# Bursts of three score tiles in a fused sigmoid attention and SiLU layer, with weighted counting of the work between them

## The chip, the cores and the metric

The kernel runs on one core of one Trainium2 chip. The metric is the device time of one execution in microseconds, the median of several runs. A profile of one execution gives the rows quoted below. Its engines are TensorE (PE, with its weight loads as PEld), VectorE (DVE), ScalarE (ACT), GpSimd (POOL) and SyncE (SP), whose queue issues DMAs.

## The reference

Two layers one after the other, in float32 at the borders. Attention has 8 batches, 12 heads, 448 positions and 64 columns per head; its weights are a sigmoid in place of a softmax. The second layer has 3,584 rows, 768 model columns and 2,048 hidden columns.

```python
scores = scale * np.matmul(q, k.transpose(0, 1, 3, 2)) - np.log(S)
attn = 1.0 / (1.0 + np.exp(-scores))
attn_out = np.matmul(attn, v)
x = attn_out.transpose(0, 2, 1, 3).reshape(B * S, H * D)
h = x @ w_in
g = h * (1.0 / (1.0 + np.exp(-h)))
out = g @ w_out
```

## The kernel before

The code writes every engine's order out by hand: the order of the Python calls is the order in each engine's queue, and TensorE, VectorE, ScalarE and the DMA queues each take their own instructions in that order. Tiles come from pools with a fixed number of buffers, and the waits between engines follow from who reads and writes them.

**Attention.** Heads are worked in 24 groups (three per batch, `g` from 0 to 23) of four heads. A group has 7 chunks, so there are 168 units `(g, ch)`; unit `n` belongs to group `n // 7`. `scores(g, ch)` (L170) issues eight 64x64 matmuls, two rounds of four that run side by side, into a score tile of two PSUM banks (pool `ps_sc`, two buffers), and one sigmoid over both banks on ScalarE into `attnT` (pool of 12). `values(g)` (L194) multiplies all seven `attnT` of a group with `v`: 28 matmuls in seven rounds, into two single banks (pool `ps_1`, four buffers). VectorE then empties these into `xT` (L219), and `after_values` starts later loads and queues the next rows.

**Rows to be transposed.** The scores need `k` and `q` with the head's columns on the partitions. Groups 0 to 5 are transposed on TensorE (`pe_transpose`). Groups 6 to 8 go by `dma_transpose` (L159) out of the h steps of batch 1. For group 9 and later, `after_values(g)` puts `(g + 3, "k")` and `(g + 3, "q")` into the list `later`, and `rows_if_any` (L467) takes one entry: VectorE copies the rows into another order (L163), and SP's queue issues the transposing DMA (L164) into `qkT`. With a `q` entry it also starts the load of a later group's k and q on POOL's queue.

**The second layer** is a stream of small steps, made by generators. `moe_h(b)` runs 16 h units for batch `b`; a unit is six 128x128 matmuls over 448 columns into one single bank (L236), a sigmoid `tsig` on ScalarE (L248) and a multiply on VectorE into `gTr` (L249). `out_set` (L289) makes two row blocks by two of the output with seven products in place of eight; a product is eight matmuls over 384 columns (L307). VectorE makes four sums and differences of blocks ahead (`S`) and adds the products up in `osb` (L315). The first product, M1, is emptied by ScalarE (L322). Two stores go to SP's queue after the sixth product and two after the seventh. The order is h0, h1, three sets, h2, a set, h3, three sets, and again from h4.

**The mix.** From unit 24 on, the main loop (L534) alternates bursts of two score tiles with a stretch of the stream. After the scores of a burst it runs the values of a waiting group, if there is one, and `rows_if_any`. `stretch(ns)` (L399) adds `ns` to `due` and takes steps until their counted time `done` reaches it: 189 per h step, 163 per product step. `hold` keeps a stretch going from the last h unit of a batch until M1 of the set behind it has been emptied. `paces` (L532) gives the time of a stretch by stage, `n // 21`. At unit 42 a stretch of 21,500 runs h1 through. What is left of the stream after the last burst runs as a dense tail.

## Time and profile before

| | |
|---|---|
| median of 3 runs | 382.31 us (382.2 to 382.5) |
| profiled execution | 382.75 us, span 381.0 |
| score matmuls, L177 | 672, busy 50.4 us, 362 ns each |
| values matmuls, L208 | 672, busy 37.9 us, 349 ns each |
| h matmuls, L236 | 768, busy 153.2 us, 353 ns each |
| sigmoid of a score tile, L184 | 168, busy 158.9 us |
| sigmoid `tsig`, L248 | 128, busy 68.2 us, 545 ns each |
| multiply into `gTr`, L249 | 128, busy 78.1 us, 623 ns each |
| additions into `osb`, L315 | 70 and 42, 555 and 552 ns each |
| M1's emptying, L322 | 14, 491 ns each |
| loads of q, k and v rows, POOL's queue | 112 KB each, 5.8, 5.5 and 4.8 us to landing |
| transposing DMAs into `qT`, SP's queue | 18, 6.2 us to landing (2.9 to 11.5) |
| stores of `osb`, SP's queue | 54, 2.9 us to landing |

Matmuls overlap in the array, so the duration of one is longer than the distance from one to the next; the distances come from the lengths of whole runs of matmuls in the chain of waits. A group's line names where the code issues it. "To landing" counts from the issue of a DMA to its last byte's arrival.

### The profile page before, as it was taken

The page shows a single profiled execution, that of the slowest core. Times are in us where ns is not written, and L with a number is a line of the kernel's source. Part 1 is how long each engine was busy: PE and PEld are TensorE (multiplying, and loading weights), DVE is VectorE, ACT ScalarE, POOL GpSimd, SP SyncE. Part 2 cuts the span into 40 slices and gives each one's busy share as a digit, 9 for nine tenths or more (in the row PEclk, how much of TensorE's full clock was granted, in tenths as well). Part 3 has the DMA queues.
Part 4 walks back from the last instruction along what each step waited for, and adds up shares of the span by engine and source line. Part 5 has one row for each costly group of instructions (what it writes and reads, how often), then busy time and mean ns, then how long its engine had stood idle before and what let it go on. Part 6 is the DMA issues. An engine that isn't in the chain of part 4 may idle for free.

```text
span 381.0 us, 7663 instructions
## 1 busy us (share of the span) xinstructions
PE 372.2 (98%) x3083; PEld 186.9 (49%) x3083; DVE 233.8 (61%) x415; ACT 240.0 (63%) x328; POOL 92.9 (24%) x158
## 2 busy tenths in 40 slices
PE   7999999999999999999999999999999999999995
PEld 2444445545554445444555444544455444555663
DVE  2446646996565666556767547735857446656773
ACT  4998886758777875778444686577774787044000
POOL 8855326202752323121311303101100000000000
PEclk9999999999999999999999999999999999999999
DMA  7999999974999936937939859535346300110233
GB/s 112 180 188 204 205 203 181 155 103 101 166 236 232 141 51 97 184 47 75 152 68 191 96 112 122 56 101 74 48 77 105 83 3 2 41 41 2 75 92 83
DMA packets 66403, 42.71 MB, mean 112 GB/s; under 512 B 37056, under 2 KB 62912, under 8 KB 66368
## 3 DMA queue, kind: packets, MB, share of 16 engines
q0 software_dynamic: 28032, 22.69, 42.7%
q1 hardware_dynamic: 38112, 19.31, 28.2%
q8 instruction: 24, 0.39, 0.4%
q10 hardware_dynamic: 224, 0.23, 0.2%
q14 instruction: 11, 0.09, 0.1%
HBM read 45.61 MB, written 11.01 MB: 149 GB/s over the span
## 4 chain that ended last, share of the span: by engine, by line
PE 80%; DMA 12%; DVE 2%; ACT 2%; POOL 1%; issue 1%; DVEq 0%
PE po L307 34%; PE ph L236 29%; PE psc L177 9%; PE pav L208 6%; DMA w_in_sb<-in_moe_w_in_dram 6%; DMA w_out_sb<-in_moe_w_out_dram 5%; DVE gTr L249 1%; DMA ks<-in_k_dram 1%; ACT attnT L184 1%; DMA vf<-in_v_dram 1%; DVE T L278 1%; POOL qf L78 1%; PE pw L135 1%; POOL kf L78 0%; ACT qr L138 0%
## 5 line engine op out<-in xcount | busy, mean ns | idle before, releaser
L184 ACT ACTIVATE attnT<-psc,bias_s 128x896 f16<-128x896 f32 x168 | 158.9, 1016 | 53.3 <-PE psc L177 53.2
L236 PE MATMUL ph<-xT,w_in_sb 128*128 128x448 f16 x768 | 153.2, 353 | 0.0
L249 DVE TENSOR_TENSOR gTr<-ph,tsig 128x448 f16<-128x448 f32 x128 | 78.1, 623 | 72.0 <-ACT tsig L248 71.4
L236 PEld LDWEIGHTS <-w_in_sb 128*128 128x128 f16 x768 | 71.9, 98 | 75.7 <-issue 12.9
L248 ACT ACTIVATE tsig<-ph 128x448 f16<-128x448 f32 x128 | 68.2, 545 | 47.8 <-PE ph L236 46.2
L78 POOL DMA_DIRECT2D vf<-in_v_dram x48 | 28.7, 613 | 140.7 <-PE pav L208 140.2
L307 PEld LDWEIGHTS <-S 128*128 128x128 f16 x448 | 42.3, 98 | 33.9 <-issue 6.8
L315 DVE SCALAR_TENSOR_TENSOR osb<-po,osb 128x384 f32<-128x384 f32 x70 | 37.7, 555 | 25.1 <-PE po L307 24.5
L177 PE MATMUL psc<-qT,kT 64*64 64x448 f16 x672 | 50.4, 362 | 2.5 <-ACT attnT L184 1.2
L219 DVE TENSOR_SCALAR xT<-pav 128x448 f16<-128x448 f32 x48 | 27.7, 619 | 30.3 <-PE pav L208 30.3
L307 PE MATMUL po<-T,S 128*128 128x384 f16 x224 | 40.6, 327 | 0.1
L307 PEld LDWEIGHTS <-gTr 128*128 128x128 f16 x304 | 28.7, 98 | 23.4 <-issue 5.2
L307 PE MATMUL po<-w_out_sb,S 128*128 128x384 f16 x224 | 39.9, 326 | 0.0
L208 PE MATMUL pav<-attnT,vf 64*64 64x448 f16 x672 | 37.9, 349 | 0.4 <-DVE gTr L249 0.4
L78 POOL DMA_DIRECT2D qf<-in_q_dram x48 | 28.9, 612 | 38.1 <-DVE qr L163 16.9
L307 PE MATMUL po<-w_out_sb,gTr 128*128 128x384 f16 x192 | 34.7, 327 | 0.0
L177 PEld LDWEIGHTS <-kT 64*64 64x64 f16 x672 | 15.0, 104 | 32.8 <-issue 30.9
L78 POOL DMA_DIRECT2D kf<-in_k_dram x48 | 28.9, 612 | 7.0 <-DVE kr L163 4.4
L208 PEld LDWEIGHTS <-vf 64*64 64x64 f16 x672 | 20.2, 107 | 12.4 <-issue 1.9
L315 DVE SCALAR_TENSOR_TENSOR osb<-po,m 128x384 f32<-128x384 f32 x42 | 23.2, 552 | 4.1 <-PE po L307 2.5
L322 ACT ACTIVATE m<-po 128x384 f32<-128x384 f32 x14 | 6.9, 491 | 23.7 <-PE po L307 23.7
L307 PE MATMUL po<-T,gTr 128*128 128x384 f16 x112 | 21.4, 326 | 0.0
(40 smaller groups left out, 131.0 us busy)
## 6 DMA issues: line engine op xcount, KB each, us to landing
out_dram<-osb SPq DMA_DIRECT2D x54, 192.0 KB, 2.9
qf<-in_q_dram POOLq DMA_DIRECT2D x48, 112.0 KB, 5.8
vf<-in_v_dram POOLq DMA_DIRECT2D x48, 112.0 KB, 4.8
kf<-in_k_dram POOLq DMA_DIRECT2D x46, 112.0 KB, 5.5
w_in_sb<-in_moe_w_in_dram POOLq DMA_DIRECT2D x4, 768.0 KB, 10.5
w_out_sb<-in_moe_w_out_dram POOLq DMA_DIRECT2D x4, 768.0 KB, 17.0
kT<-kr SPq DMA_TRANSPOSE x18, 5.6
qT<-qr SPq DMA_TRANSPOSE x18, 6.2
```

The costliest lines, as they stand in the source:

```text
L78: nc.gpsimd.dma_start(flat[name, g][half * HP : (half + 1) * HP, :, c0:c1].rearrange("p i c d -> p i (c d)"), source[name][b, h0 : h0 + 2] ...
L135: nc.tensor.matmul(pw, dummy[:, :P], dummy, start=True, stop=True)
L177: nc.tensor.matmul(psc[own, j, :S], qkT["k", g][rows, ch, own], qkT["q", g][rows, :, own], start=True, stop=True,)
L184: nc.scalar.activation(attnT[g, ch], psc[:, :, :S], AF.Sigmoid, bias=bias_s, scale=QKSCALE)
L208: nc.tensor.matmul(pav[half][j * D : (j + 1) * D, :S], flat["v", g][own, j, ch, :], at[own, j, :], start=(ch == 0), stop=(ch == NCH - 1),)
L219: nc.vector.tensor_scalar_mul(xT[b][:, half * NQ + iq, :], pav[half][:, :S], SX)
L236: nc.tensor.matmul(ph[:, :S], w_in_sb[:, cc, fc * P : (fc + 1) * P], xT[b][:, cc, :], start=(at == 0), stop=(at == NCC - 1),)
L248: nc.scalar.activation(tsig, ph[:, :S], AF.Sigmoid, bias=0.0, scale=ISX)
L249: nc.vector.tensor_mul(gTr[:, fc, (b % 2) * S : (b % 2) * S + S], ph[:, :S], tsig)
L307: nc.tensor.matmul(po[:, :NO2], a[:, fc, :], w[:, fc, :], start=(fc == 0), stop=(fc == NHC - 1))
L315: nc.vector.scalar_tensor_tensor(out=o, in0=po, scalar=sign, in1=x, op0=ALU.mult, op1=ALU.add)
L322: nc.scalar.activation(m1, po, AF.Copy, scale=ISX)
```

## The change

Bursts from unit 42 on have three tiles in stages 2 and 4 to 7 and two in stage 3, and two tiles whenever a group's values are waiting. In a burst of three the first tile goes to two single banks out of `ps_1`, with a sigmoid for each, the second and third to `ps_sc`, and the third's sigmoid is put off: it is issued behind the next `tsig` or M1's emptying, or once a stretch has taken steps of more than 1,300 ns, or at the stretch's end. `stretch` counts a step by a weight: 0.72 in the h stages from batch 2 on, 1.28 in the sets. `hold` begins an h unit earlier from batch 2 on. The paces change, and a stretch is scaled by the tiles of its burst. Rows are no longer transposed in a burst that has a waiting group, unless more than one entry is queued at its start.

```diff
-    def scores(g, ch):
+    late = []
+
+    def late_sigmoid():
+        while late:
+            to, psc = late.pop()
+            nc.scalar.activation(to, psc, AF.Sigmoid, bias=bias_s, scale=QKSCALE)
+
+    def scores(g, ch, banks=None, put_off=False):
         attnT[g, ch] = p12.tile([P, 2, S], F16, tag="attnT", name="attnT")
-        psc = ps_sc.tile([P, 2, 512], F32, tag="pssc", name="psc")
+        if banks is None:
+            psc = ps_sc.tile([P, 2, 512], F32, tag="pssc", name="psc")
+            banks = [psc[:, j] for j in range(2)]
+            parts = [(attnT[g, ch], psc[:, :, :S])]
+        else:
+            parts = [(attnT[g, ch][:, j], banks[j][:, :S]) for j in range(2)]
...
-        nc.scalar.activation(
-            attnT[g, ch], psc[:, :, :S], AF.Sigmoid, bias=bias_s, scale=QKSCALE
-        )
+        if put_off:
+            late.extend(parts)
+            return
+        for to, psc in parts:
+            nc.scalar.activation(to, psc, AF.Sigmoid, bias=bias_s, scale=QKSCALE)
+
+    def single_banks():
+        return [ps_1.tile([P, 512], F32, tag="ps1", name="psc1") for _ in range(2)]
...
     def h_unit(b, fc):
-        hold = b > 0 and fc == NFC - 1
+        weight = H_WEIGHT if b > 1 else 1.0
+        hold = b > 1 and fc >= NFC - 2 or b == 1 and fc == NFC - 1
...
         nc.scalar.activation(tsig, ph[:, :S], AF.Sigmoid, bias=0.0, scale=ISX)
+        late_sigmoid()
...
+    H_WEIGHT, SET_WEIGHT = 0.72, 1.28
...
     def out_set(a1, rows1, a2, rows2, last=False):
+        weight = SET_WEIGHT
...
         nc.scalar.activation(m1, po, AF.Copy, scale=ISX)
+        late_sigmoid()
...
     def stretch(ns):
         due += ns
+        since = 0
         while done < due or hold:
             step_ns = next(stream, None)
             if step_ns is None:
                 break
-            done += step_ns
+            done += step_ns * weight
+            since += step_ns
+            if since > 1300:
+                late_sigmoid()
+        late_sigmoid()
...
-    paces = {1: 1600, 2: 2000, 3: 2550, 4: 3400, 5: 3400, 6: 3000, 7: 3000}
+    TILES = {2: 3, 3: 2, 4: 3, 5: 3, 6: 3, 7: 3}
+    paces = {1: 1600, 2: 2400, 3: 2550, 4: 3500, 5: 3300, 6: 3100, 7: 2900}
+    def burst(n, tiles):
+        new = units[n : n + (tiles if not waiting else 2)]
+        for i, u in enumerate(new):
+            single = i == len(new) - 3
+            scores(*u, single_banks() if single else None, len(new) == 3 and i == 2)
+        rows = not waiting or len(later) > 1
+        values_if_any()
+        if rows:
+            rows_if_any()
+        waiting.extend(g for g, ch in new if ch == NCH - 1)
+        return len(new)
...
+    values_if_any()
+    stretch(21500)
+    n = 2 * NT_B
+    while n < len(units):
+        ns = paces[n // NT_B]
+        tiles = burst(n, TILES[n // NT_B])
+        n += tiles
+        stretch(ns * tiles / 2)
```

More of the change, by code (lines that the diff above doesn't have):

```diff
@@ L177, in scores @@
                 nc.tensor.matmul(
-                    psc[own, j, :S],
+                    banks[j][own, :S],
                     qkT["k", g][rows, ch, own],
@@ L228 @@
     hold = False
+    weight = 1.0
     def h_unit(b, fc):
-        nonlocal hold
-        hold = b > 0 and fc == NFC - 1
+        nonlocal hold, weight
+        weight = H_WEIGHT if b > 1 else 1.0
+        hold = b > 1 and fc >= NFC - 2 or b == 1 and fc == NFC - 1
         ph = ps_1.tile([P, 512], F32, tag="ps1", name="ph")
@@ L289, in out_set @@
     def out_set(a1, rows1, a2, rows2, last=False):
-        nonlocal hold
+        nonlocal hold, weight
+        weight = SET_WEIGHT
         lo, hi = slice(0, NHC), slice(NHC, NFC)
@@ L530 @@
             do(*what)
-    paces = {1: 1600, 2: 2000, 3: 2550, 4: 3400, 5: 3400, 6: 3000, 7: 3000}
-    stretch(paces[1])
-    for n in range(NT_B + 3, len(units), 2):
-        burst = units[n : n + 2]
-        if n == 2 * NT_B:
-            values_if_any()
-            stretch(21500)
-        for u in burst:
-            scores(*u)
-        values_if_any()
-        rows_if_any()
-        for g, ch in burst:
-            if ch == NCH - 1:
-                waiting.append(g)
+    TILES = {2: 3, 3: 2, 4: 3, 5: 3, 6: 3, 7: 3}
[11 more added lines that the diff above has]
+        return len(new)
+    stretch(paces[1])
+    for n in range(NT_B + 3, 2 * NT_B, 2):
+        burst(n, 2)
         if n in (24, 30):
@@ L549 @@
             transposes(4 + (n - 26) // 6, "q")
-        stretch(paces[1] if 1 not in ready else paces[n // NT_B])
+        stretch(paces[1])
+    values_if_any()
[6 more added lines that the diff above has]
+        stretch(ns * tiles / 2)
     for g in waiting:
```

## The prediction

> **What bounds the kernel now.** I read the busy times first, then the chain of waits in order of time, then the timeline around the transposing transfers, and last their landing times by stretch of the run.

> ```profile
> span 381.0 us, 7663 instructions
> ...
> PE 372.2 (98%) x3083; PEld 186.9 (49%) x3083; DVE 233.8 (61%) x415; ACT 240.0 (63%) x328; POOL 92.9 (24%) x158
> ```

> TensorE has work in 98% of the span; VectorE and ScalarE are idle over a third of it. Whatever adds idle time to TensorE adds it to the end. The chain of waits in order of time (start, duration, what) shows the rhythm, and the densest stretches at the end:

> ```profile
> 196.07 1.32 PE pav L208 x28
> 197.40 3.52 PE po L307 x21
> 200.92 0.50 PE psc L177 x8
> 201.42 3.52 PE po L307 x21
> ...
> 331.31 18.16 PE ph L236 x96
> 349.47 27.32 PE po L307 x168
> ```

> From these: one product matmul takes 27.32/168 = 0.163 us, one h matmul 18.16/96 = 0.189, one round of four 64x64 matmuls 1.32/7 = 0.189. A cycle of one burst of two score tiles and 21 products lasts 0.50 + 3.52 = 4.02 us, of which 21 x 0.163 + 2 x 0.189 = 3.79 are matmuls. The remaining **0.23 us** is what one change to 64x64 tiles and back costs. The 18-matmul cycles of the h stages (0.50 + 3.51) give the same 0.23.

> **Fewer bursts: a gain.** From unit 42 on there are 126 units. Before: 126/2 = 63 bursts. After, I walk the loop by hand: due grows by pace x tiles / 2, each h step counts 189 x 0.72 and each set step 163 x 1.28, a burst has two tiles whenever a group waits for its values, and the hold runs through two h units and M1. That gives 26 bursts of three and 24 of two, so 50. One pair of these (78 and 80, behind the hold after h2) has no step between them and shares one change. So 14 changes fewer: 14 x 0.23 = **3.2 us gained**. The steps in the tail are the same matmuls in another place: nothing.

> **ScalarE.** A split tile costs two activations of 0.533 us (68.2/128, tsig's row) in place of one of 0.946 (158.9/168): 26 x 0.12 = 3.1 us on an engine with 141 us idle. The tightest cycle is a burst of three and 17 products, 0.80 + 2.77 = 3.57 us, against 2 x 0.533 + 2 x 0.946 + about 0.15 for M1 = 3.1: it fits, so I take nothing. The put-off sigmoid holds its score bank until the next burst, at least 2.6 us on; tsig or M1 waits behind two tiles, as before. The one stall of TensorE behind scores in steady work (at 144.64, M1 and then four sigmoids in line, 0.65 us) shrinks by about **0.2**: the burst there now has 1.32 us of values between its two pairs of tiles.

> **PSUM.** The split tile takes two of the four single banks, and the accumulation that follows the burst's own gets the bank of the one just before. That one has 0.80 + 1.13 (h) or 0.80 + 1.30 us (product) to be emptied; tsig 0.545 + the VectorE multiply 0.623, or two additions of 0.555, need about 1.4 with the start. It is hidden; with a row copy (0.61) and a difference (0.68) ahead on VectorE it could miss by some 0.4. I take 0, with 3 us (a quarter of 26) as the upper end, and no gain.

> **The transposed rows: a loss.** What is moved and not named in the change is the row transposing. A group's k and q rows are copied by VectorE (L163) and transposed by a DMA on SP's queue (L164), one name per burst, k first. Before, every burst does one, so q follows k by one burst and lands long ahead. After, a burst with a waiting group skips it unless two or more entries are queued, and there are 2.5 to 3 bursts per group in place of 3.5. Entries pile up and q goes out one burst before its group's first scores. My walk gives a lead from q's burst to its first score of 14.5 to 25.4 us before (groups 9 to 23). After, with 0.23 per burst, 0.189 per tile and the steps between:
> - group 9: q at burst 58; its first unit, 63, is third in burst 61: 3 x 0.189 + 0.23 + 17 x 0.163 + 2 x 0.189 = 3.9 us
> - 10: burst 66 to 70, 6.3; 11: burst 72 to second in 76, 8.4; 12 to 15: over 14
> - 16: burst 107 to third in 110, 5.1; 17: 115 to second in 118, 8.0
> - 18: burst 123 to first in 126, 3.6; 19: 128 to third in 131, 5.5; 20: 136 to second in 139, 8.0
> - 21: burst 144 to first in 147, 4.4; 22: 149 to third in 152, 4.6; 23: 157 to second in 160, 7.0

> What a lead must cover, in the timeline (start, duration, engine, line):

> ```profile
> 103.45 0.57 PE L177 MATMUL psc<-qT,kT 64*64 64x448 f16 x8
> ...
> 104.56 3.01 SPq L300 DMA_DIRECT2D out_dram<-osb  x4
> ...
> 105.89 0.61 DVE L163 COPY qr<-qf 128x896 f16<-128x896 f16 x1
> ...
> 107.67 1.58 SPq L164 DMA_TRANSPOSE qT<-qr  x1
> ...
> 231.61 0.57 PE L177 MATMUL psc<-qT,kT 64*64 64x448 f16 x8
> ...
> 232.84 0.61 DVE L163 COPY qr<-qf 128x896 f16<-128x896 f16 x1
> ...
> 233.47 1.22 SPq L164 DMA_TRANSPOSE qT<-qr  x1
> ```

> From the burst's start to the issue: 1.9 us in the second case, 4.2 in the first, where four stores stand ahead on SP's queue. Over the groups it is 0.9 to 1.9 without stores (I take 1.4) and 2.8 to 4.2 behind four; groups 9 and 16 copy just behind a set's first two stores (2.2), 17 behind all four (2.9). From issue to landing, the answers for qT in the stretches 90 to 121, 180 to 220, 225 to 250 and 255 to 295 us:

> ```profile
> DMA to landing us min/median/max: 6.6/7.6/10.5
> DMA to landing us min/median/max: 6.1/6.3/6.8
> DMA to landing us min/median/max: 3.4/3.9/4.3
> DMA to landing us min/median/max: 2.9/3.8/4.0
> ```

> Stall = issue + landing (median of the stretch) - lead. Group 9: 2.2 + 7.6 - 3.9 = 5.9. Group 10: 1.4 + 7.6 - 6.3 = 2.7. Group 11 (median 7.1 over 90 to 130): 0.1. Group 16: 2.2 + 6.3 - 5.1 = 3.4. Group 17: 2.9 + 6.3 - 8.0 = 1.2. Group 18: 1.4 + 3.9 - 3.6 = 1.7. Group 21: 1.4 + 3.8 - 4.4 = 0.8; group 22: 0.6; 19, 20 and 23: none. Together **16.4 us lost**. TensorE takes its matmuls in order, so all the h and product steps behind those scores wait, and nothing later has slack to give it back. k goes out earlier, 8.8 us or more before its scores; behind the evictions of a values burst its issue takes 3.7 and its landing 3.8 to 5.2: no stall. The k and q loads move with it, but have 38 us or more for 5.8: nothing.

> Bounds: with the lowest landing and issue of each stretch (0.9; 1.5 behind two stores) the stalls are 4.2 + 1.2 + 2.5 + 0.9 + 0.7 = 9.5; with the highest (10.5 for groups 9 and 10, 7.6 for 11, 6.8 for 16 to 18, then 4.3 and 4.0; issue 1.9, or 3.4 and 4.2 behind stores) about 34; with the shortest landing anywhere, 2.9, and the quickest issue, 0.7.

> **Sum.** Profiled execution 382.75 us (span 381.0 and 1.75 around it): - 3.2 - 0.2 + 16.4 = 395.75. The median of the runs, 382.31, lies 0.44 below it, so I predict **395.3**.

> **Rivals.**
> (a) The transfers land in time. If in the new places each q lands in the 2.9 us seen once in a quiet stretch, 0.7 us of stall is left: 382.3 - 3.4 + 0.7 = 379.6, faster. It decides where landings stay under about 3.3 us all along, since the stalls then add up to less than the 3.4 gained. For: the rows of a group are 128x896 f16, 229 KB, and late in the run DMA is busy 41% (225 to 325 us). Against: in the stretch of groups 9 and 10 the shortest is 6.6. Chance 0.08. [...]
> (b) A long stall slows the matmuls behind it. The first eight matmuls of the run (128x512, from 1.46 us) take 3.60 us, 0.45 each, and later ones of that shape come at 0.23: the array starts at half rate and needs some 3.7 us. If group 9's stall, or 16's too, brings that back, each costs half of 3.7: 395.3 + 1.9 to 3.7 = 397.2 to 399. Against: no idle time in the trace past 10 us exceeds 1 us, so it can't show it. Chance 0.20. [...]
> (c) Banks or ScalarE run late too: the 3 us above on top, 398.3. Chance 0.07.
> (d) The stalls are real but about as large as the gain, 3 to 4 us (each landing some 3 us under its stretch's median: group 9 at 2.9, 16 at 0.4): 382. Chance 0.05.
> The forecast itself has 0.60.

> **How the numbers follow.** The forecast's own range is 388.4 (stalls 9.5) to 402; with (b) and (c) above it I go to 405, and below it to 386.5, which leaves out (a), (d) and the far end of the high bound. About 0.2%, 0.8 us, is what a measurement of this kernel tells from no change. Faster comes from (a) and a part of (d), 0.09; same from (d), 0.02; slower is the rest, 0.89.

> **What would show it.** Right: waits of TensorE's score matmuls or weight loads on the DMA of qT, some seven of them, the longest at group 9 (near 106 us) and group 16, together about 16 us; TensorE's busy share near 95%; transpositions of q issued one burst ahead of their group. The cycles of three tiles without a stall should still cost 0.23 over their matmuls. Wrong: no such waits and a span below 379; or stalls that end on ScalarE or VectorE instead, which would put the loss on the bursts of three themselves.

## The result and the profile after

The changed kernel takes **405.1 us** (median of 6 runs, 403.1 to 409.8) against 382.4 before (382.2 to 382.7): 1.0585 times as long, interval 1.0561 to 1.0609. The ratio leaves out the longest run, which counts as slow at 1.7% above the fastest; the median of the other five is 404.7 us. That longest run, 409.83 us with a span of 408.1, is the profiled one. It is compared with the span of 381.0 before. The others left no trace: how their 403.1 to 407.1 us divide is not shown.

From the page of the changed kernel: the busy times, then TensorE's row of 40 slices of the span (each digit its busy share in tenths) and the row PEclk, the clock that TensorE was granted, in tenths of full speed:

```profile
span 408.1 us, 7693 instructions
...
PE 379.8 (93%) x3083; PEld 193.4 (47%) x3083; DVE 235.1 (58%) x415; ACT 243.6 (60%) x354; POOL 93.3 (23%) x158
...
PE   7999999999397999999996999769999999999995
...
PEclk9999999999979999999998999897999999999999
```

The same 3,083 matmuls are busy 7.6 us longer, and TensorE is idle in 28 us in place of 9. There are holes in the row of TensorE, and notches at them in the row of the clock, which shows 9 in every slice before. The view of who waited for whom, TensorE's lines only (waited for: total, times, longest), names the holes:

```profile
PE psc L191 <- DMA qT<-qr: 19.1, 6, 6.5
...
PE psc L191 <- ACT attnT L202: 1.1, 4, 0.4
```

Before, no wait on `qT`'s transposing DMA stood there. The line for the scores was:

```profile
PE psc L177 <- ACT attnT L184: 1.2, 4, 0.5
```

(Lines have moved: L177, L208, L236 and L307 of the kernel before are L191, L227, L257 and L333 after.) The chain of waits in order of time around the first hole and a later one (start, duration, what):

```profile
86.37 0.69 PE psc L191 x12
87.06 2.87 PE po L333 x17
...
102.95 8.91 DMA qT<-qr
111.86 0.14 issue
111.99 0.59 PE psc L191 x4
112.58 5.19 PE po L333 x17
...
256.34 3.98 DMA qT<-qr
260.45 0.85 PE psc L191 x8
261.30 2.66 PE pav L227 x28
...
267.68 7.44 DMA qT<-qr
275.25 0.59 PE psc L191 x4
275.84 9.15 PE ph L257 x34
```

Two things are to be seen. The score matmuls start 0.13 us after the transposing DMA of their group's q has landed. And what follows is slow: 17 product matmuls take 5.19 us in place of 2.87 (the same count at 87.06), 28 values matmuls 2.66 in place of 1.32, 34 h matmuls 9.15 in place of 34 x 0.189 = 6.4. The granted clock is 0.50 for part or all of these stretches (the last section has the windows). A score tile, by the counts here, is four 64x64 matmuls in one round: 672 matmuls for 168 tiles, and not eight to a tile.

From the starts of successive matmuls, TensorE stood 6.6 us for group 9, 2.1 for 10, 4.1 for 16, 0.8 for 17, 3.0 for 18, 3.3 for 19 and 0.2 for 22: 20.1. The matmuls at half rate took 10.5 us more than at full. With 3.4 for the fewer bursts, as forecast (the experiments find 2.8), 381.0 + 20.1 + 10.5 - 3.4 = 408.2, against 408.1 measured.

### The profile page after: what moved, and what is told of

Read it like the earlier page. It is cut to its first block, busy times and chain, and to the rows that moved or that the text cites. A ratio compares the mean times of both kernels' runs of the same rounds, so it can differ in the third digit from the quotient of the medians.

```text
span 408.1 us, 7693 instructions
## 1 busy us (share of the span) xinstructions
PE 379.8 (93%) x3083; PEld 193.4 (47%) x3083; DVE 235.1 (58%) x415; ACT 243.6 (60%) x354; POOL 93.3 (23%) x158
## 4 chain that ended last, share of the span: by engine, by line
PE 78%; DMA 14%; ACT 2%; POOL 2%; DVE 1%; issue 1%; DVEq 0%; ACTq 0%; POOLq 0%
PE ph L257 34%; PE po L333 29%; DMA qT<-qr 10%; PE psc L191 8%; PE pav L227 7%; DMA w_in_sb<-in_moe_w_in_dram 3%; ACT attnT L202 2%; DMA vf<-in_v_dram 1%; POOL kf L78 1%; POOL qf L78 1%; DVE osb L341 0%; DVE qr L163 0%; PE ptrq L148 0%; POOL vf L78 0%; PE ptrk L148 0%
## 5 line engine op out<-in xcount | busy, mean ns | idle before, releaser
L202 ACT ACTIVATE attnT<-psc,bias_s 128x896 f16<-128x896 f32 (+1 forms) x168 | 138.0, 900 | 55.4 <-PE psc L191 55.4
L257 PE MATMUL ph<-xT,w_in_sb 128*128 128x448 f16 x768 | 154.4, 358 | 0.2 <-DMA w_in_sb<-in_moe_w_in_dram 0.2
L257 PEld LDWEIGHTS <-w_in_sb 128*128 128x128 f16 x768 | 73.9, 99 | 76.6 <-issue 12.4
L191 PE MATMUL psc<-qT,kT 64*64 64x448 f16 x672 | 50.0, 366 | 21.0 <-DMA qT<-qr 19.1
L333 PEld LDWEIGHTS <-S 128*128 128x128 f16 x448 | 43.3, 100 | 35.8 <-issue 10.6
L333 PE MATMUL po<-T,S 128*128 128x384 f16 x224 | 43.2, 343 | 0.0
L191 PEld LDWEIGHTS <-kT 64*64 64x64 f16 x672 | 16.7, 105 | 50.4 <-issue 47.7
L227 PE MATMUL pav<-attnT,vf 64*64 64x448 f16 x672 | 40.2, 365 | 0.4 <-DVE gTr L271 0.4
L333 PE MATMUL po<-w_out_sb,S 128*128 128x384 f16 x224 | 39.9, 327 | 0.0
L333 PEld LDWEIGHTS <-gTr 128*128 128x128 f16 x304 | 28.7, 98 | 23.6 <-issue 5.7
L333 PE MATMUL po<-w_out_sb,gTr 128*128 128x384 f16 x192 | 35.9, 332 | 0.0
L175 ACT ACTIVATE attnT<-psc,bias_s 128x896 f16<-128x896 f32 x26 | 26.5, 1018 | 7.8 <-PE psc L191 7.8
L227 PEld LDWEIGHTS <-vf 64*64 64x64 f16 x672 | 21.9, 111 | 12.3 <-issue 1.9
```

Source lines behind the costliest of these rows:

```text
L175: nc.scalar.activation(to, psc, AF.Sigmoid, bias=bias_s, scale=QKSCALE)
L191: nc.tensor.matmul(banks[j][own, :S], qkT["k", g][rows, ch, own], qkT["q", g][rows, :, own], start=True, stop=True,)
L202: nc.scalar.activation(to, psc, AF.Sigmoid, bias=bias_s, scale=QKSCALE)
L227: nc.tensor.matmul(pav[half][j * D : (j + 1) * D, :S], flat["v", g][own, j, ch, :], at[own, j, :], start=(ch == 0), stop=(ch == NCH - 1),)
L257: nc.tensor.matmul(ph[:, :S], w_in_sb[:, cc, fc * P : (fc + 1) * P], xT[b][:, cc, :], start=(at == 0), stop=(at == NCC - 1),)
L333: nc.tensor.matmul(po[:, :NO2], a[:, fc, :], w[:, fc, :], start=(fc == 0), stop=(fc == NHC - 1))
```

## The experiments

Each was run beside the kernel before on the same chip (382.4 to 382.7); ratios are to it.

**Rows in every burst.** The changed kernel without its rule for the rows:

```diff
-        rows = not waiting or len(later) > 1
+        rows = True
```

> The changed kernel with rows transposed in every burst, as before the change. Theory (late q rows stall the scores, the stalls halve the clock): q is again issued 11 us or more ahead of its group's scores, so the 19 to 20 us of waits on qT and the 10.5 us of half clock both go, and what is left is the gain of fewer bursts: 382.4 - 3.4 = 379.0 us, clock 1.00. Rival (the bursts of three, the put-off sigmoid or the weights cost of themselves): over 382.4, with TensorE waiting for ScalarE or VectorE.

379.99 us, ratio 0.9938 (0.9924 to 0.9953), clock 1.00. The whole loss is gone, and the rest of the change is faster than before, by 2.4 us where 3.4 was expected. TensorE's waits in this kernel, all of 0.3 us or more:

```profile
PE pw L135 <- DVE bias_s L454: 1.5, 1, 1.5
PE psc L191 <- ACT attnT L202: 1.1, 4, 0.4
PE pav L227 <- DVE gTr L271: 0.4, 1, 0.4
PE psc L191 <- ACT qT L138: 0.3, 1, 0.3
```

None is on a DMA.

**The rule alone.** The kernel before, with the rule and nothing else:

```diff
+        rows = not waiting or len(later) > 1
         values_if_any()
-        rows_if_any()
+        if rows:
+            rows_if_any()
```

> The kernel before with the new row rule alone (no rows in a burst that has a waiting group, unless two are queued). Theory: with 3.5 bursts per group two of them are always free for k and q, q keeps 11.9 us or more of lead, nothing stalls: 382.4 us, within 0.2%. Rival (the rule is harmful by itself): waits on qT and 385 us or more.

383.0 us, ratio 1.0015 (1.0006 to 1.0025), no wait on `qT` in the trace. One of its ten runs took 390.8 us; it left no trace, and its cause is open. So neither half does the harm: the rule costs some 0.6 us with bursts of two and 25 us with bursts of three. It is the two together.

**Both rows in the next burst.** The rule stays, and the burst after a values burst takes two entries:

```diff
-        rows = not waiting or len(later) > 1
+        rows = not waiting
         values_if_any()
         if rows:
             rows_if_any()
+            rows_if_any()
```

> The changed kernel with no rows in a burst that has a waiting group, and both k and q of a group in the next burst. Theory: what did the harm is that entries were taken more slowly than they came; q now leads its scores by 11.4 us or more, no waits on qT, 380.0 us. Rival (leaving the values bursts out is harmful of itself, or two copies in a burst hold VectorE and with it the banks): 382 or more.

379.6 us, ratio 0.9921 (0.9907 to 0.9934). Leaving out the bursts with a waiting group is harmless; taking entries more slowly than they come was not. The profiled execution (380.6, the longest of six) still has one wait on `qT`:

```profile
PE psc L191 <- DMA qT<-qr: 1.3, 1, 1.3
```

**One late group.** Rows in every burst, but group 9's q kept back until the burst at unit 58, where the changed kernel issues it:

```diff
+        kept_back = later.pop(0) if later[:1] == [(9, "q")] and n < 58 else None
         rows_if_any()
+        if kept_back:
+            later.insert(0, kept_back)
```

> The version with rows in every burst, in which the q rows of group 9 alone are kept back until the burst at unit 58, where the changed kernel issues them. Theory: one stall of 6.6 us (issue 1.6, landing 8.9, less the lead of 3.9) and one or two windows of half clock behind it (1.5 or 3.0 us): 380.0 + 6.6 + 2.3 = 388.9 us, 385 to 392 as the landing falls; clock 0.98 to 0.99. Rival (the loss in the changed kernel is spread over the bursts and not tied to late rows): about 380.

391.85 us, ratio 1.0241 (1.0227 to 1.0255), clock 0.986 to 0.987 in all runs. One late transfer costs 11.9 us over the 379.99 of rows in every burst. The mechanism is the expected one, and the landing was longer than the 8.9 us that were put in: q landed 10.9 us after its issue, TensorE stood 9.2 us, and the product matmuls behind it lost 2.1. These make 11.3 of the 11.6 us by which the spans differ (389.8 and 378.2). The chain there:

```profile
104.22 10.88 DMA qT<-qr
115.10 0.14 issue
115.24 0.59 PE psc L191 x4
115.83 4.71 PE po L333 x17
```

**Is it the idle time that halves the clock?** Extra matmuls on constant data, ahead of the first scores of a group, take the place of idle time:

```diff
+        if ch == 0:
+            keep_busy(WARM.get(g, 0))
```

First in the changed kernel, at five groups (`WARM = {9: 24, 10: 7, 16: 14, 18: 10, 19: 11}`).

> The changed kernel with 24, 7, 14, 10 and 11 extra matmuls of 128x512 on constant data ahead of the first scores of groups 9, 10, 16, 18 and 19; they fill some 14 us of the 19 us in which TensorE waits for qT. Theory that idle time brings the half clock: the waits end when they did, the clock stays at 1.00, and the 10.5 us of slow matmuls go: about 395 us. Rival (the clock falls for another reason, or the slow stretch is hidden): 405 us or more, since the extra matmuls only add.

402.1 us (399.5 to 403.0), ratio 1.0507 (1.0467 to 1.0546): 3 us less than the changed kernel, not 10. The clock is up to 0.996 to 1.00 from 0.97 to 0.985. In the profiled execution the mean granted clock of 0.996 over 401.2 us leaves some 1.6 us (0.004 x 401.2) to the half rate in place of 10.5, but TensorE still waited for `qT`:

```profile
PE psc L194 <- DMA qT<-qr: 6.4, 4, 3.2
```

These 6.4 us stand beside some 14 of extra matmuls, together more than the 19.1 of waits that they replace. The sizes were taken from one execution, the longest. The result lies between theory and rival, and decides nothing by its time alone. So it was put to the kernel with one late group, first with 20 extra matmuls.

> The same with 20 extra matmuls of 128x512 ahead of group 9's first scores, 4.3 us of the stall. Theory that a mostly idle window brings the half clock: the stall is as long, the clock stays at 1.00, 386.6 us, some 2 us under the version without them. Rival (no effect of the idle time on the clock): the same time or more, clock below 0.99.

393.0 us, ratio 1.0267 (1.0242 to 1.0292): no gain. 20 were too few. The wait on `qT` still left 6.1 us idle behind the extra matmuls, and the mean granted clock over 103 to 123 us was 0.83. This run doesn't decide between the two. With 40:

> The version in which group 9's q rows alone are late, with 40 extra matmuls of 128x512 ahead of its first scores, 8.6 us, so that at most 3 us of the wait are idle even if q lands 12 us after its issue. Theory that idle time brings the half clock: clock 1.00 all along, no slow products behind the wait, and the time falls by the 2.1 us that they cost in the version without extra matmuls, if q lands no later: 389.8 us; with a landing later by 1.5 us, 391.3. Rival: products behind the wait still at half rate, 0.32 us each.

390.4 us, ratio 1.0201 (1.0186 to 1.0216), clear of the version without them (1.0227 to 1.0255). Busy times and clock over 103 to 121 us, first for one late group, then with 40 extra matmuls (length, then PE, PEld, DVE, ACT and POOL busy, the granted clock, DMA share, GB/s):

```profile
103.00:121.00 18.00, 8.94 (x58) 4.25 (x60) 5.34 (x10) 5.97 (x10) 5.85 (x10) 0.72 1.14 169
```

```profile
103.00:121.00 18.00, 17.42 (x125) 8.42 (x124) 5.84 (x11) 7.07 (x9) 6.14 (x11) 1.00 1.06 161
```

The chip gets the same late rows (q landed after 11.2 us) and does more work, and it is done 1.5 us earlier, with the array busy for 17.42 of the 18.00 us at a granted clock of 1.00, against 8.94 at 0.72.

**Where the gain comes from.** Rows in every burst, and two tiles in every burst:

```diff
-    TILES = {2: 3, 3: 2, 4: 3, 5: 3, 6: 3, 7: 3}
+    TILES = {2: 2, 3: 2, 4: 2, 5: 2, 6: 2, 7: 2}
```

> The changed kernel with rows in every burst and two tiles in every burst, the weights and hold kept: 63 bursts from unit 42 on in place of 50. Theory: the gain is in the number of changes of tile size, 13 x 0.23 = 3.0 us, so this one is 3 us over the version with bursts of three, about 382.0 to 382.5. Rival (the gain is in the weights and the hold): as fast as that version, about 379.

385.4 us, ratio 1.0083 (1.0067 to 1.0100): 5.4 over the bursts of three, not 3. The trace has 63 bursts in place of 50, and 62 changes of tile size in place of 50, since two pairs of bursts have only values between them; by the price of one, 12 x 0.23 = 2.8 us. The rest is in the waits:

```profile
PE psc L191 <- ACT attnT L202: 4.1, 10, 0.7
```

That is 3.0 us more than the 1.1 with bursts of three. Behind a hold, two bursts follow with one product matmul between them (at 236 us), and all four tiles want the same two score buffers while M1 and four sigmoids (0.49 and 3.69 us) are in line on ScalarE. With bursts of three the first tile has banks of its own. So the weights and the longer hold are no gain by themselves: with bursts of two they are 3.0 us over the kernel before. Bursts of three without them were not run.

**The put-off sigmoid.** Rows in every burst, `put_off` always `False`:

> The version with rows in every burst, with the third tile's sigmoid issued at once instead of behind the next tsig or M1. Theory: tsig then waits behind three tiles (3.0 us) in place of two, its bank is asked for again four units on, at 4.4 us or later, and is free at about 4.6: 380.0 us, at most 1 us more. Rival (the putting-off carries the gain): 382 or more, with TensorE waiting for VectorE's multiply.

379.7 us, ratio 0.9917 (0.9905 to 0.9930), its interval overlapping that of rows in every burst. The putting-off does nothing that can be measured.

**Stage 3 in threes.** Rows in every burst, `3: 3` in `TILES`:

> The version with rows in every burst, with bursts of three in stage 3 too: three bursts fewer, and the two bursts without a step between them behind the hold after h2 fall apart. Theory: 380.0 - 3 x 0.23 + 0.23 - up to 0.5 (the M1 stall) = 379.0 to 379.6. Rival (ScalarE is the bound in stage 3): 380.5 or more.

379.9 us, ratio 0.9930 (0.9918 to 0.9943): the same as in twos, and above the 379.0 to 379.6 expected. The expectation counted three bursts fewer; the trace has 48 in place of 50, and with the pair apart that is one change of tile size fewer, 0.2 us. Against it, the waits of score matmuls for ScalarE come to 1.7 us (0.9 and 0.8 in two lines of the view) in place of 1.1.

## Why the prediction was right, and where not

**The way and the cause** were right: the rows, which the change doesn't speak of, go out one burst ahead of their scores, and 405.1 in place of 382.4 is their doing; without that, the change is a gain. The forecast of 395.3 was 9.8 us short. The result lies at the upper end of the range: the median of all six is 0.1 above 405, that of the five behind the ratio 0.3 below. That it fits so nearly is in part luck. The room above 402 was made for (b) and (c), of which (c) didn't come and (b) came at almost three times its upper price in the profiled execution; and 402 is not worked out from the high bound of the stalls, which comes to some 31 us by its own terms, and not 34.

**The stalls, by group** (forecast and measured, in us): 9: 5.9 and 6.6; 10: 2.7 and 2.1; 11: 0.1 and 0; 16: 3.4 and 4.1; 17: 1.2 and 0.8; 18: 1.7 and 3.0; 19: 0 and 3.3; 21: 0.8 and 0; 22: 0.6 and 0.2. Together 16.4 and 20.1. The leads worked out by hand held, within 0.4 us where a stall shows them. The sizes of two terms were off. For group 18 VectorE copied 1.85 us after the burst's start, so that the issue came at 2.5 and not 1.4. For group 19 the landing, taken as the 3.9 us median of a quiet stretch of the kernel before, was 7.4: the answer for `qT` between 266 and 270 us after the change reads

```profile
DMA to landing us min/median/max: 7.4/7.4/7.4
```

The change moved the traffic beside this landing too: the DMA share (busy time over that of 16 engines) was 1.29 from this issue to its landing, against 1.14 and 0.98 for the q rows at 233 and 245 us before, which landed in 4.3 and 3.4. k's rows of the same group had been issued 2 us earlier, in a values burst behind a stall, and landed after 6.7 us.

**The half clock** was the step that failed: it stood outside the sum as rival (b), with a chance of 0.20, at one or two stalls and 1.9 to 3.7 us. It happened at five of seven stalls and cost 10.5 us in the profiled execution, the largest part of its miss (409.8 against 395.75; the longer stalls are 3.7). The other runs had it too: their granted clock was 0.972 to 0.985, against 0.970 there and 1.00 with rows in every burst. The price of one was about right (1.6 to 2.9 us each); what was wrong was to count only the longest stalls as able to bring it on. The trace before, where TensorE's longest idle time later than 10 us was 0.5 us, could not show it. Two of the five falls came behind windows in which the array had worked for 37 and 39% of the time (last section), and the half rate lasted 3.4 or 6.8 us, where (b) took 3.7 from the start of the run. With 40 extra matmuls in place of group 9's idle time the granted clock over 103 to 121 us was 1.00, against 0.72 without them: there, idle time is the cause.

**The gain** was forecast as 3.4 us. From unit 42 on the changes of tile size did fall from 64 to 50, by the forecast 14. A cycle of three tiles and 17 product matmuls takes 0.69 + 2.87 = 3.56 us, which is 0.22 over its matmuls (17 x 0.163 + 3 x 0.189), as forecast. With rows in every burst 2.4 us are left by the medians, 2.8 by the spans (381.0 and 378.2); the stall behind M1 went from 0.65 to 0.51. Two bursts of two wait 0.2 us each for ScalarE (97.8 and 273.2 us), and one burst of three (101.5 us) takes 0.94 us in place of 0.69, for no cause that was traced; together about the 0.6 that the spans lack.

**The other rivals.** (a), q landing in time, would have needed 3.3 us all along; the landings that stalled TensorE took 2.9 to 8.9. (c), banks or ScalarE late of themselves, would show in the version with rows in every burst and doesn't. (d) had stalls of 3 to 4 us, and they were 20.1.

## What to carry to other kernels

Count, for every queue of prepared work, entries made and entries taken per round when the rounds become fewer: a transfer issued "one burst ahead" was early only because bursts were many. Put the lead from issue to first use beside the longest landing in that traffic, not beside the median: group 19's took 7.4 us, where 3.9 was put in. And count what a stall on TensorE costs behind it: in the profiled execution of the changed kernel 20.1 us of waiting cost 30.6. Its stalls of 2.1 us and more came with half clock behind them, those of 0.8 and less did not.

## What the runs showed of the hardware

```profile
127.50:130.91 3.41, 1.33 (x23) 0.74 (x24) 0.96 (x2) 0.96 (x2) 0.00 (x0) 1.00 1.28 220
130.91:134.33 3.42, 3.42 (x29) 1.48 (x18) 1.16 (x2) 1.49 (x2) 1.26 (x3) 0.50 0.40 139
```

The array worked 1.33 of 3.41 us in the first, 39%, stood for 2.1, and had half clock in the whole of the second, though it was busy all through it. The windows before the other four falls in mid-run, at 110.43, 219.66, 260.62 and 274.27 us, had 0, 0, 0.44 and 1.27 us of work. With the traces before and after cut into such windows, counted from the first rise of the clock, no fall came behind one with more than 39%; the emptiest of these at full clock had 1.67 us of work (49%, the kernel before, 375.10 to 378.52 us) and 1.91 (56%, the changed kernel, 103.61 to 107.02), and none lay between. The half clock lasted for one window, 3.4 us, where the array was busy in it for 3.23 us or more, and for two, 6.8 us, where it was busy for 1.86 and 2.43 us in the first and all through the second. The stalls of 0.5 us before (at 144.2 us) and 0.8 after (group 17, at 238.3 us) brought no fall.

The traces before and after have 72 transposing DMAs of 229 KB on SP's queue. None landed in less than 2.9 us. Where the DMA share was under 0.5 from issue to landing, in four of them, each took 2.9 us; where it was 1.2 or more, in 30, the median was 6.9 us, between 5.0 and 11.5.
